# Attention and token mixer on one core: transposes in the scores' PSUM banks, half buffers for x and y, weight conversion in three stages

## The chip, the cores and the metric

The kernel runs on one core of one Trainium2 chip. The core has a matrix engine (TensorE, PE in the views), which reads SBUF and writes the eight banks of PSUM; VectorE (DVE) and ScalarE (ACT), which read PSUM and SBUF; GpSimd (POOL), which works in SBUF; and SyncE (SP), which here only issues DMAs. Each engine works through its own list of instructions in order. The metric is the device time of one execution in microseconds (us), and lower is better. Before the change it was 1676.6 us, the median of three runs (1676.05 to 1679.02).

## The reference

```python
def _attn_ref(q, k, v, g_q, g_k):            # q, k, v: (8, 12, 448, 64)
    def rmsnorm(x, g):
        return x / np.sqrt(np.mean(x * x, axis=-1, keepdims=True) + 1e-06) * g
    q_n, k_n = (rmsnorm(q, g_q), rmsnorm(k, g_k))
    scores = 1.0 / np.sqrt(q.shape[-1]) * np.matmul(q_n, k_n.transpose(0, 1, 3, 2))
    attn = np.exp(scores - np.max(scores, axis=-1, keepdims=True))
    attn = attn / (np.sum(attn, axis=-1, keepdims=True) + 1e-09)
    return np.matmul(attn, v)

# x: the heads side by side, (8, 448, 768); w_tok1 (448, 256), w_tok2 (256, 448),
# w_ch1 (768, 1536), w_ch2 (1536, 768)
def _moe_ref(x, w_tok1, w_tok2, w_ch1, w_ch2):
    xt = x.transpose(0, 2, 1)
    u = x + (np.maximum(xt @ w_tok1, 0.0) @ w_tok2).transpose(0, 2, 1)
    return u + np.maximum(u @ w_ch1, 0.0) @ w_ch2
```

All arithmetic is in float32. The four weight matrices arrive as float64, so the kernel first turns each into float32 by integer and float operations on the two 32-bit halves of every number.

## The kernel before

Work is in 8 batches. A batch's attention is 6 pairs of heads, and a pair has two steps of two 112-row chunks of keys each. For a pair, `load_qk` brings q and k, `norm_pair` makes the reciprocal root mean squares `rs` (ScalarE's squares, L553; VectorE's sums, L556; GpSimd's power, L561), `scale` multiplies q by them, and `trans_qk` (L212, L214) transposes q and k on TensorE into a PSUM bank and copies them out with ScalarE as `qkT`. A step computes four score tiles (L227), takes their exponentials on ScalarE (L233), multiplies those of the step before with v (L284) and adds the exponentials up (L270 on GpSimd, L274 on VectorE). `denominator` sums over partitions on TensorE (L298), and VectorE divides (L310 to L316). The result of a batch is `uT`, six blocks of 128 channels by 448 positions.

The mixer of a batch turns `uT` into `x` (`trans_x`, L364, copies L369 on ScalarE and L371 on VectorE by turns), multiplies with w_tok1 (`tok1`, L379) and w_tok2 (`tok2`, L387), adds to `uT` (L392), multiplies with w_ch1 (`ch1`, L403, 72 matmuls) and w_ch2 (`ch2`, L416, 72), adds again (L421), turns the result back into `y` (`trans_y`, L428, L430) and stores each half of `y` with a DMA that ScalarE issues (L435).

PSUM is split in three pools: four banks for score tiles (`ps_S`), two for products with v (`ps_O`), and two (`ps_M`) for everything else: transposes, denominators, and all the mixer's tiles. `x` and `y` share one buffer of a whole batch (`x_pool`, one slot, L358 to L436). So the copies into the next batch's `x` wait until the last half of `y` is stored.

The weights come in chunks of up to 128 by 256 numbers. `convert_first` (L136) splits a chunk on VectorE (L148, L149) and goes on with it on ScalarE (L151, L152). One item later `convert_last` (L154) finishes it on VectorE (L168, L170) and GpSimd (L172). The load of the chunk three items ahead is issued behind that (L126).

The order on TensorE, VectorE, ScalarE and GpSimd is written out by hand: `merge` (L23) weaves lists of items by their costs. In the first stage the attention of batch 0 (and two steps of batch 1) is woven with the first 15 conversion items; after that the attention of batch b + 1 is woven with the mixer of batch b, in batch 0 with the other conversions too (L474 to L483). The last batch's mixer has no attention beside it. Two versions of the program are built, and a test of g_q and g_k chooses one on the chip (L598). With these inputs it is the one that does not subtract a maximum.

```python
    m_tile = lambda: ps_M.tile([P, 512], F32, name="m_ps", tag="M")
    BEFORE = len(first) + NC + 1
    x_pool = pool("x_pool", 1)
```

## Time and profile before

| | |
|---|---|
| time, median of 3 runs | 1676.6 us (1676.05 to 1679.02) |
| the profiled execution | 1678.31 us, its span 1676.5 us |
| TensorE busy | 1539.9 us (92%) |
| VectorE, ScalarE, GpSimd busy | 473.2, 493.9, 368.6 us (28, 29, 22%) |
| mean granted TensorE clock | 0.97 of 2.4 GHz |
| from HBM, to HBM | 53.74 MB, 11.01 MB |

The page cuts the span in 40 slices of 42 us. TensorE is nearly full in most of them, and the three other engines are busy for half their time and more in the first seven, where the weights are converted. A busy share says where an engine works, not which wait ends last. For that, the views of waits and the timelines are read by stage: 15 to 124 us (attention of batch 0 beside conversions), 124 to 340 us (mixer of batch 0 beside attention and conversions), and from 340 us on (seven batches of about 200 us, the last shorter). A float32 matmul leaves two records in the trace, so the counts of TensorE's records are twice those of its matmuls.

### The profile page before, as it was taken

How to read it: one execution, taken by the hardware profiler on the slowest of the kernel's cores; microseconds unless marked ns; L12 is line 12 of the kernel's file. 1: busy time of each engine (PE TensorE's matmuls, PEld its weight loads, DVE VectorE, ACT ScalarE, POOL GpSimd, SP SyncE). 2: the span in 40 equal slices, each digit the busy share in tenths (PEclk: the TensorE clock that was granted, in tenths of full speed). 3: DMA queues.
4: the chain of work that ended last, by engine and by line, in shares of the span. 5: the costliest groups of instructions: out<-in, count | busy, mean ns of one | idle time of the engine just before them, and what ended most of it. 6: DMA issues, size and time to landing. Idle time of an engine off the chain costs nothing.

```text
span 1676.5 us, 13714 instructions
## 1 busy us (share of the span) xinstructions
PE 1539.9 (92%) x5248; PEld 734.3 (44%) x5248; DVE 473.2 (28%) x831; ACT 493.9 (29%) x890; POOL 368.6 (22%) x234
## 2 busy tenths in 40 slices
PE   5768998989998999989999899998999899998998
PEld 2234443444444444444444444444444444444554
DVE  4556866421222221122112221222122121111000
ACT  5554655323222222222222223222322222211100
POOL 5554554211211121111111211211122111100000
PEclk9879999999999999999999999999999999999999
DMA  5223433111002000110011101011100200000001
GB/s 121 79 78 98 123 105 109 53 33 29 22 17 61 17 22 17 44 39 17 17 28 39 33 17 28 23 33 33 28 22 18 61 17 12 6 17 17 0 0 34
DMA packets 119886, 65.73 MB, mean 39 GB/s; under 512 B 91716, under 2 KB 109892, under 8 KB 119812
## 3 DMA queue, kind: packets, MB, share of 16 engines
q1 hardware_dynamic: 111138, 53.53, 12.4%
q10 hardware_dynamic: 8674, 11.24, 2.2%
q8 instruction: 43, 0.70, 0.2%
q14 instruction: 31, 0.25, 0.0%
HBM read 53.74 MB, written 11.01 MB: 39 GB/s over the span
## 4 chain that ended last, share of the span: by engine, by line
PE 83%; DVE 6%; ACT 4%; DMA 3%; POOL 2%; issue 2%; SPq 0%; ACTq 0%; DVEq 0%; POOLq 0%
PE m_ps L416 26%; PE m_ps L403 24%; PE s_ps L227 9%; PE o_ps L284 9%; PE m_ps L379 5%; PE m_ps L387 4%; PE m_ps L298 2%; DMA out_dram<-y 2%; PE m_ps L364 2%; PE m_ps L212 1%; DVE uT L421 1%; ACT qkT L214 1%; POOL rs L561 1%; PE m_ps L428 1%; DVE es L274 1%
## 5 line engine op out<-in xcount | busy, mean ns | idle before, releaser
L416 PE MATMUL m_ps<-h,wc_sb 128*128 128x448 f32 x1152 | 455.8, 547 | 7.4 <-DVE uT L421 7.1
L403 PE MATMUL m_ps<-uT,wc_sb 128*128 128x448 f32 x1152 | 448.6, 543 | 4.1 <-ACT h L407 2.2
L403 PEld LDWEIGHTS m_ps<-uT,wc_sb 128*128 128x128 f32 x1152 | 213.8, 190 | 221.8 <-issue 203.5
L416 PEld LDWEIGHTS m_ps<-h,wc_sb 128*128 128x128 f32 x1152 | 213.8, 191 | 221.4 <-issue 207.5
L233 ACT ACTIVATE e<-s_ps,rs 112x448 f32<-112x448 f32 x384 | 211.9, 633 | 196.1 <-PE s_ps L227 196.1
L270 POOL TENSOR_TENSOR es<-e 112x896 f32<-112x896 f32 x48 | 100.2, 2087 | 765.5 <-PE m_ps L298 647.2
L227 PE MATMUL s_ps<-qkT 64*112 64x448 f32 x768 | 180.0, 590 | 27.6 <-ACT qkT L214 27.6
L561 POOL TENSOR_TENSOR rs<-ms,mhalf_c 112x16 f32<-112x16 f32 (+1 forms) x49 | 144.5, 2949 | 223.7 <-DVE ms L560 216.6
L284 PE MATMUL o_ps<-e,vt 112*64 112x448 f32 x768 | 170.6, 566 | 0.0
L310 DVE STREAM_TRANSPOSE dt<-m_ps 128x448 f32<-128x448 f32 x48 | 31.2, 650 | 452.3 <-PE m_ps L298 452.3
L407 ACT ACTIVATE h<-m_ps 128x448 f32<-128x448 f32 x96 | 52.1, 542 | 352.5 <-PE m_ps L403 352.5
L274 DVE TENSOR_TENSOR es<-es,e 112x896 f32<-112x896 f32 x96 | 113.7, 1185 | 82.5 <-ACT e L233 77.9
L421 DVE TENSOR_TENSOR uT<-uT,m_ps 128x448 f32<-128x448 f32 x48 | 29.8, 621 | 346.6 <-PE m_ps L416 346.4
L214 ACT ACTIVATE qkT<-m_ps,g_t 128x448 f32<-128x448 f32 x96 | 60.0, 631 | 220.7 <-PE m_ps L212 220.6
L227 PEld LDWEIGHTS s_ps<-qkT 64*112 64x112 f32 x768 | 64.4, 181 | 126.4 <-issue 93.6
L284 PEld LDWEIGHTS o_ps<-e,vt 112*64 112x64 f32 x768 | 47.9, 140 | 115.2 <-issue 115.2
L556 DVE TENSOR_REDUCE ms<-sq 112x16 f32<-112x1024 f32 (+1 forms) x49 | 58.5, 1196 | 138.0 <-ACT sq L553 138.0
L172 POOL TENSOR_TENSOR wc_sb<-m_t,e_t 128x256 f32<-128x256 f32 x72 | 62.5, 875 | 123.2 <-DVE e_t L170 122.1
L387 PE MATMUL m_ps<-w_sb,h 128*128 128x448 f32 x192 | 80.4, 564 | 8.3 <-DVE uT L392 4.6
L379 PE MATMUL m_ps<-x,w_sb 112*128 112x384 f32 x256 | 86.9, 497 | 0.0
L364 PE MATMUL m_ps<-ident,uT 128*112 128x128 f32 x192 | 40.7, 378 | 41.7 <-ACT x L369 36.8
L430 ACT COPY y<-m_ps 112x512 f32<-112x512 f32 x48 | 28.0, 585 | 168.4 <-PE m_ps L428 168.4
(45 smaller groups left out, 817.2 us busy)
## 6 DMA issues: line engine op xcount, KB each, us to landing
raw<-in_moe_w_ch_dram SPq DMA_DIRECT2D x72, 256.0 KB, 2.7
vt<-in_v_dram SPq DMA_DIRECT2D x48, 224.0 KB, 2.6
out_dram<-y ACTq DMA_DIRECT2D x16, 672.0 KB, 4.4
qk<-in_q_dram SPq DMA_DIRECT2D x92, 112.0 KB, 2.8
qk<-in_k_dram SPq DMA_DIRECT2D x92, 112.0 KB, 2.8
raw<-in_moe_w_tok_dram SPq DMA_DIRECT2D x4, 224.0 KB, 4.2
raw<-in_moe_w_tok_dram SPq DMA_DIRECT2D x2, 256.0 KB, 2.8
wc_sb<-in_q_dram SPq DMA_DIRECT2D x4, 112.0 KB, 3.8
```

Of the source, the lines that this page charges most:

```text
L214: nc.scalar.mul(st["qkT", p][:, i, :], ps[:, 0:S], g_t[:, i:i + 1])
L227: nc.tensor.matmul(out=ps[0:R, 0:S], lhsT=qkT[a * D:(a + 1) * D, 1, kc * R:(kc + 1) * R], rhs=qkT[a * D:(a + 1) * D, 0, :], start=True, st ...
L233: nc.scalar.activation(out=e[0:R, a, i, :], in_=pss[a][0:R, 0:S], func=AF.Exp, scale=st["rs", p][0:R, r:r + 1])
L270: nc.gpsimd.tensor_tensor(out=es[0:R], in0=e[0:R, :, 0, :], in1=e[0:R, :, 1, :], op=ALU.add)
L274: nc.vector.tensor_tensor(out=es[0:R], in0=es[0:R], in1=e[0:R, :, i, :], op=ALU.add)
L284: nc.tensor.matmul(out=o[a * D:(a + 1) * D, 0:S], lhsT=vt[0:R, a, kc * D:(kc + 1) * D], rhs=e[0:R, a, i, :], start=(kc == 0), stop=(kc == ...
L364: nc.tensor.transpose(ps[0:R, c * P:(c + 1) * P], st["uT", b][:, j, c * R:(c + 1) * R], ident[:, :])
L379: nc.tensor.matmul(out=ps[:, 0:HC], lhsT=w1_sb[0:R, c, jc * P:(jc + 1) * P], rhs=st["x"][0:R, c, cs], start=(c == 0), stop=(c == NS - 1))
L387: nc.tensor.matmul(out=ps[:, 0:S], lhsT=st["h1", jc][:, cc * P:(cc + 1) * P], rhs=w2_sb[:, jc].rearrange("p c r -> p (c r)"), start=(jc == ...
L403: nc.tensor.matmul(out=ps[:, 0:S], lhsT=wc1_sb[:, cc, f * P:(f + 1) * P], rhs=st["uT", b][:, cc, :], start=(cc == 0), stop=(cc == NC - 1))
L416: nc.tensor.matmul(out=ps[:, 0:S], lhsT=wc2_sb[:, f, cc * P:(cc + 1) * P], rhs=st["h2"][:, f, :], start=(f == 0), stop=(f == NF - 1))
L561: nc.gpsimd.tensor_tensor(out=rs[0:R, w], in0=ms[0:R, w], in1=self.mhalf_c[0:R].to_broadcast([R, (hi - lo) * n]), op=ALU.pow)
```

## The change

Transposes of q and k, of x and of y take their PSUM tiles from the four score banks (`s_tile`) instead of the two shared ones. `x` and `y` become tiles of half the channels, in two slots: half 0 of x, half 1 of x, half 0 of y, half 1 of y take them by turns. `trans_x` and `trans_y` share a helper, `turn`. The mixer now transposes the three blocks of a half and runs that half of tok1 before it goes on to the other half. In the last batch each block of 128 channels of `y` is stored by itself. A conversion is spread over three items: VectorE's split, an item later ScalarE's part, an item later VectorE's end and GpSimd's product. `cv_pool` has four slots instead of three, and loads are issued two items ahead instead of three.

```diff
@@ -60,12 +60,12 @@
     HC = C // 2
     HN = NS // 2
     assert S % NS == 0 and R <= P and 2 * D == P and H % 2 == 0 and NC == NPAIR
-    assert DT % P == 0 and C % P == 0 and DC % P == 0 and HC <= 512 and S <= 512
+    assert DT % P == 0 and C % P == 0 and DC % P == 0 and HC <= 512 and HC % P == 0 and S <= 512

     pool = lambda name, bufs, **kw: ctx.enter_context(tc.tile_pool(name=name, bufs=bufs, **kw))
     const = pool("const", 1)
     raw_pool = pool("raw_pool", 4)
-    cv_pool = pool("cv_pool", 3)
+    cv_pool = pool("cv_pool", 4)
     pre.qk_pool = pool("qk_pool", 3)
     pre.sq_pool = pool("sq_pool", 1)
     pre.st_pool = pool("st_pool", 4)
@@ -75,7 +75,7 @@
     es_pool = pool("es_pool", 1)
     rd_pool = pool("rd_pool", 2)
     uT_pool = pool("uT_pool", 2)
-    x_pool = pool("x_pool", 1)
+    x_pool = pool("x_pool", 2)
     h1_pool = pool("h1_pool", 2)
     h2_pool = pool("h2_pool", 1)
     ps_S = pool("ps_S", 4, space=PSUM)
@@ -90,6 +90,7 @@

     st = dict(pre.st)
     m_tile = lambda: ps_M.tile([P, 512], F32, name="m_ps", tag="M")
+    s_tile = lambda name: ps_S.tile([P, 512], F32, name=name, tag="S")

@@ -144,9 +145,17 @@
         m_t = cv_pool.tile([P, WCOLS], U32, name="m_t")
         st["cv", i] = e_t, m_t
         e, m = e_t[0:rows, 0:n], m_t[0:rows, 0:n]
-        mf = m.bitcast(F32)
         nc.vector.tensor_scalar(e, hi, 0x7FF00000, None, ALU.bitwise_and)
         nc.vector.tensor_scalar(m, hi, 0x000FFFFF, None, ALU.bitwise_and)
+
+    def convert_second(i):
+        rows, src, dst, split = chunks[i]
+        if src.dtype != I64:
+            return
+        e_t, m_t = st["cv", i]
+        n = src.shape[-1]
+        e, m = e_t[0:rows, 0:n], m_t[0:rows, 0:n]
+        mf = m.bitcast(F32)

         nc.scalar.activation(out=e, in_=e, func=AF.Relu, bias=expo_c[0:rows, 0:1], scale=8.0)
         nc.scalar.activation(out=mf, in_=m, func=AF.Identity, bias=one_c[0:rows, 0:1], scale=2.0**-20)
@@ -171,17 +180,17 @@
             out=e, in0=hi, scalar=0x80000000, in1=e, op0=ALU.bitwise_and, op1=ALU.bitwise_or)
         nc.gpsimd.tensor_tensor(out=dst, in0=fold(mf), in1=fold(ef), op=ALU.mult)

-    LOADS_AHEAD = 3
-
     def weight_items(lo, hi):

         def one(i):
             if i < len(chunks):
                 convert_first(i)
-            if i:
-                convert_last(i - 1)
-            if i + LOADS_AHEAD < len(chunks):
-                weight_load(i + LOADS_AHEAD)
+            if 0 <= i - 1 < len(chunks):
+                convert_second(i - 1)
+            if i >= 2:
+                convert_last(i - 2)
+            if i + 2 < len(chunks):
+                weight_load(i + 2)
         return [(1.0, lambda i=i: one(i)) for i in range(lo, hi)]


@@ -207,7 +216,7 @@
         qk = st["qk", p]
         if i == 0:
             st["qkT", p] = qkT_pool.tile([P, 2, S], F32, name="qkT")
-        ps = m_tile()
+        ps = s_tile("t_ps")
         for c in range(NS):
             nc.tensor.transpose(
                 ps[:, c * R:(c + 1) * R], qk[0:R, i, c].rearrange("p h d -> p (h d)"), ident[0:R, 0:R])
@@ -223,7 +232,7 @@
             kc = h * HN + i
             pss = []
             for a in range(2):
-                ps = ps_S.tile([P, 512], F32, name="s_ps")
+                ps = s_tile("s_ps")
                 nc.tensor.matmul(
                     out=ps[0:R, 0:S], lhsT=qkT[a * D:(a + 1) * D, 1, kc * R:(kc + 1) * R],
                     rhs=qkT[a * D:(a + 1) * D, 0, :], start=True, stop=True)
@@ -244,7 +253,7 @@
             st["e", p, i] = e_pool.tile([P, 2, HN, S], F32, name="e")
         for c in range(NS):
             for a in range(2):
-                ps = ps_S.tile([P, 512], F32, name="s_ps")
+                ps = s_tile("s_ps")
                 nc.tensor.matmul(
                     out=ps[0:R, 0:S], lhsT=qkT[a * D:(a + 1) * D, 0, c * R:(c + 1) * R],
                     rhs=qkT[a * D:(a + 1) * D, 1, :], start=True, stop=True)
@@ -355,20 +364,25 @@

-    def trans_x(b, j):
-
-        if j == 0:
-            st["x"] = x_pool.tile([P, NS, C], F32, name="x", tag="x")
-        ps = m_tile()
+    def turn(b, j, name, by_act):
+
+        half, o = divmod(j * P, HC)
+        if o == 0:
+            st[name, half] = x_pool.tile([P, NS, HC], F32, name=name, tag="x")
+        ps = s_tile("t_ps")
         for c in range(NS):
             nc.tensor.transpose(
                 ps[0:R, c * P:(c + 1) * P], st["uT", b][:, j, c * R:(c + 1) * R], ident[:, :])
         src = ps[0:R, :].rearrange("p (c n) -> p c n", c=NS)
-        dst = st["x"][0:R, :, j * P:(j + 1) * P]
-        if j % 2:
+        dst = st[name, half][0:R, :, o:o + P]
+        if by_act:
             nc.scalar.copy(out=dst, in_=src)
         else:
             nc.vector.tensor_copy(out=dst, in_=src)
+
+    def trans_x(b, j):
+
+        turn(b, j, "x", j % 2)

     def tok1(b, jc, h):
         cs = slice(h * HC, (h + 1) * HC)
@@ -377,7 +391,7 @@
         ps = m_tile()
         for c in range(NS):
             nc.tensor.matmul(
-                out=ps[:, 0:HC], lhsT=w1_sb[0:R, c, jc * P:(jc + 1) * P], rhs=st["x"][0:R, c, cs],
+                out=ps[:, 0:HC], lhsT=w1_sb[0:R, c, jc * P:(jc + 1) * P], rhs=st["x", h][0:R, c, :],
                 start=(c == 0), stop=(c == NS - 1))
         nc.scalar.activation(out=st["h1", jc][:, cs], in_=ps[:, 0:HC], func=AF.Relu)

@@ -421,26 +435,23 @@
             nc.vector.tensor_tensor(out=uT, in0=uT, in1=ps[:, 0:S], op=ALU.add)

     def trans_y(b, cc):
-        if cc == 0:
-            st["y"] = x_pool.tile([P, NS, C], F32, name="y", tag="x")
-        ps = m_tile()
-        for c in range(NS):
-            nc.tensor.transpose(
-                ps[0:R, c * P:(c + 1) * P], st["uT", b][:, cc, c * R:(c + 1) * R], ident[:, :])
-        nc.scalar.copy(
-            out=st["y"][0:R, :, cc * P:(cc + 1) * P], in_=ps[0:R, :].rearrange("p (c n) -> p c n", c=NS))
-        half = NC // 2
-        if cc % half == half - 1:
-            cs = slice((cc + 1 - half) * P, (cc + 1) * P)
+        turn(b, cc, "y", True)
+        half, o = divmod(cc * P, HC)
+        n = P if b == B - 1 else HC
+        if (o + P) % n == 0:
+            o += P - n
             nc.scalar.dma_start(
-                out=out[b].rearrange("(p c) n -> p c n", c=NS)[:, :, cs], in_=st["y"][0:R, :, cs])
-            if cc == NC - 1:
-                st.pop(("uT", b))
+                out=out[b].rearrange("(p c) n -> p c n", c=NS)[:, :, half * HC + o:half * HC + o + n],
+                in_=st["y", half][0:R, :, o:o + n])
+        if cc == NC - 1:
+            st.pop(("uT", b))

     def mlp_items(b):
         us = lambda n, cols: n * cols * 4 / 2400
-        items = [(0.5, lambda j=j: trans_x(b, j)) for j in range(NC)]
-        items += [(us(NS, HC), lambda j=j, h=h: tok1(b, j, h)) for j in range(NJ) for h in range(2)]
+        items = []
+        for h in range(2):
+            items += [(0.5, lambda j=j: trans_x(b, j)) for j in range(h * NC // 2, (h + 1) * NC // 2)]
+            items += [(us(NS, HC), lambda j=j, h=h: tok1(b, j, h)) for j in range(NJ)]
         items += [(us(NJ, S), lambda cc=cc: tok2(b, cc)) for cc in range(NC)]
         items += [(us(NC // 2, S), lambda f=f, p=p: ch1(b, f, p)) for f in range(NF) for p in range(2)]
         early, late = items, []
@@ -458,10 +469,10 @@
     first, second, third = weight_chunks()
     chunks = first + second + third
     AHEAD = 1
-    BEFORE = len(first) + NC + 1
+    BEFORE = len(first) + NC + 2

     load_v(0)
-    for i in range(LOADS_AHEAD):
+    for i in range(2):
         weight_load(i)
     scale(0)
     trans_qk(0, 0)
@@ -476,7 +487,7 @@
     for b in range(B):
         early, late = mlp_items(b)
         if b == 0:
-            early = merge(early, weight_items(BEFORE, len(chunks) + 1))
+            early = merge(early, weight_items(BEFORE, len(chunks) + 2))
         lo = (b + AHEAD) * per + 2
         att = att_items(lo, lo + per) if b + AHEAD < B else []
         for _, fn in merge(att, early + late):
```

At the boundary between two batches (here from the second to the third) TensorE's list had, before, from the last matmuls of ch2 to the end of tok1 (L212 transposes of q and k, L428 of y, L364 of x; then L227 scores, L284 products with v, L298 denominators, L379 tok1):

```order
L416 MATMUL m_ps<-h_3328,wc_sb 128x448 x9
L212 MATMUL m_ps<-ident,qk 128x112 x4
L428 MATMUL m_ps<-ident,uT 112x128 x4
L212 MATMUL m_ps<-ident,qk 128x112 x4
L428 MATMUL m_ps<-ident,uT 112x128 x4
L364 MATMUL m_ps<-ident,uT 112x128 x24
L227 MATMUL s_ps<-qkT 112x448 x4
L284 MATMUL o_ps<-e,vt 64x448 x4
L298 MATMUL m_ps<-es,one_c 64x448 x2
L379 MATMUL m_ps<-x,w_sb 128x384 x16
```

Now the same place reads (L221 transposes of q and k, L374 those of y and of x, L236 scores, L293 products, L307 denominators, L393 tok1):

```order
L430 MATMUL m_ps<-h_3333,wc_sb 128x448 x9
L221 MATMUL t_ps<-ident,qk 128x112 x4
L374 MATMUL t_ps<-ident,uT 112x128 x4
L221 MATMUL t_ps<-ident,qk 128x112 x4
L374 MATMUL t_ps<-ident,uT 112x128 x16
L393 MATMUL m_ps<-x,w_sb 128x384 x4
L236 MATMUL s_ps<-qkT 112x448 x4
L293 MATMUL o_ps<-e,vt 64x448 x4
L307 MATMUL m_ps<-es,one_c 64x448 x2
L393 MATMUL m_ps<-x,w_sb 128x384 x4
L374 MATMUL t_ps<-ident,uT 112x128 x12
L393 MATMUL m_ps<-x,w_sb 128x384 x8
```

The transposes of y and the first three of x stand in one run of 16 instructions, a quarter of tok1 follows at once, and the last three blocks of x stand behind the attention step and the second quarter of tok1.

On VectorE the distance between the two parts of a conversion shows by the buffers' numbers. In the first stage before, with L148 and L149 the split and L168 and L170 the end:

```order
L148 TENSOR_SCALAR e_t_455<-raw_314 128x192
L149 TENSOR_SCALAR m_t_456<-raw_314 128x192
L168 SCALAR_TENSOR_TENSOR m_t_406<-raw_283,m_t_406 128x256
L170 SCALAR_TENSOR_TENSOR e_t_405<-raw_283,e_t_405 128x256
L274 TENSOR_TENSOR es_443<-es_443,e_466 112x896 x2
L148 TENSOR_SCALAR e_t_504<-raw_365 128x256
L149 TENSOR_SCALAR m_t_505<-raw_365 128x256
L168 SCALAR_TENSOR_TENSOR m_t_456<-raw_314,m_t_456 128x192
L170 SCALAR_TENSOR_TENSOR e_t_455<-raw_314,e_t_455 128x192
```

Now, with L177 and L179 the end:

```order
L323 STREAM_TRANSPOSE rd_532<-rc_530 128x448
L325 TENSOR_TENSOR uT_326<-o_ps_472,rd_532 128x448
L148 TENSOR_SCALAR e_t_535<-raw_445 128x192
L149 TENSOR_SCALAR m_t_536<-raw_445 128x192
L177 SCALAR_TENSOR_TENSOR m_t_437<-raw_358,m_t_437 128x192
L179 SCALAR_TENSOR_TENSOR e_t_436<-raw_358,e_t_436 128x192
L567 TENSOR_REDUCE ms_549<-sq_548 112x16
L571 TENSOR_SCALAR ms_549<-ms_549 112x16
L148 TENSOR_SCALAR e_t_576<-raw_486 128x256
L149 TENSOR_SCALAR m_t_577<-raw_486 128x256
L177 SCALAR_TENSOR_TENSOR m_t_478<-raw_396,m_t_478 128x256
L179 SCALAR_TENSOR_TENSOR e_t_477<-raw_396,e_t_477 128x256
```

Before, chunk 455 was split in one item and ended in the next (L168 and L170 on `e_t_455`). Now the first item ends chunk 436, and the chunk split there, 535, is not yet ended in the second item, which ends 477.

## Rows read from the trace of the kernel before

**Rows 1.** The page, part 2: busy tenths and granted clock in 40 slices.

```profile
PE   5768998989998999989999899998999899998998
PEclk9879999999999999999999999999999999999999
```

**Rows 2.** TensorE's waits, 15 to 124 us: total us, times, longest.

```profile
PE s_ps L227 <- ACT qkT L214: 27.6, 7, 6.6
```

**Rows 3.** Windows, first stage: busy us (records) of each engine, PEclk, DMA, GB/s.

```profile
26.58:116.70 90.12, 61.89 (x265) 22.58 (x265) 52.46 (x100) 48.96 (x92) 51.51 (x32) 0.85 0.31 83
...
54.06:70.46 16.40, 10.07 (x45) 3.58 (x45) 10.24 (x21) 8.79 (x17) 11.92 (x8) 0.84 0.36 90
```

**Rows 4.** Timeline of one pair: start, us, engine, line, operation, [idle before <-releaser].

```profile
46.12 1.76 PE L227 MATMUL s_ps<-qkT 64*112 64x448 f32 x8
...
49.77 0.26 DVE L148 TENSOR_SCALAR e_t<-raw 128x192 uint32<-128x192 uint32 x1
...
50.06 0.45 ACT L151 ACTIVATE e_t<-e_t,expo_c 128x192 uint32<-128x192 uint32 x1 [4.56 <-DVE e_t L148]
...
50.77 2.19 ACT L233 ACTIVATE e<-s_ps,rs 112x448 f32<-112x448 f32 x4
...
52.83 1.17 ACT L214 ACTIVATE qkT<-m_ps,g_t 128x448 f32<-128x448 f32 x2
...
54.06 2.34 PE L227 MATMUL s_ps<-qkT 64*112 64x448 f32 x8 [3.61 <-ACT qkT L214]
```

**Rows 5.** TensorE's waits, 124 to 340 us.

```profile
PE m_ps L212 <- ACT qkT L214: 9.0, 3, 6.0
PE m_ps L428 <- DVE uT L421: 5.4, 2, 5.1
PE m_ps L387 <- DVE uT L392: 4.6, 2, 2.4
```

**Rows 6.** Windows, two stretches at the low clock.

```profile
294.00:301.00 7.00, 4.41 (x12) 2.91 (x13) 5.83 (x14) 3.27 (x9) 2.69 (x3) 0.51 0.22 56
256.50:263.30 6.80, 3.94 (x9) 2.31 (x10) 3.29 (x9) 2.86 (x6) 2.46 (x3) 0.50 0.50 135
```

**Rows 7.** TensorE's waits, 340 us to the end.

```profile
PE m_ps L364 <- ACT x L369: 35.4, 7, 5.6
PE m_ps L212 <- ACT qkT L214: 8.7, 12, 0.7
PE m_ps L416 <- DVE uT L421: 6.1, 22, 0.3
PE m_ps L387 <- ACT qkT L214: 3.6, 5, 0.7
PE m_ps L428 <- DVE uT L421: 2.5, 8, 0.3
```

**Rows 8.** Timeline, a batch boundary, with a score matmul ahead of it.

```profile
524.48 1.76 PE L227 MATMUL s_ps<-qkT 64*112 64x448 f32 x8
...
537.44 1.44 PE L364 MATMUL m_ps<-ident,uT 128*112 128x128 f32 x8
...
538.20 0.58 ACTq L435 DMA_DIRECT2D out_dram<-y  x1
...
543.14 0.58 ACT L369 COPY x<-m_ps 112x512 f32<-112x512 f32 x1 [4.96 <-DMA out_dram<-y]
...
543.77 3.84 PE L364 MATMUL m_ps<-ident,uT 128*112 128x128 f32 x16 [4.90 <-ACT x L369]
...
547.55 2.98 PE L227 MATMUL s_ps<-qkT 64*112 64x448 f32 x8
...
552.86 10.59 PE L379 MATMUL m_ps<-x,w_sb 112*128 112x384 f32 x32
```

**Rows 9.** The page, part 6: DMAs, KB each, median us to landing.

```profile
vt<-in_v_dram SPq DMA_DIRECT2D x48, 224.0 KB, 2.6
out_dram<-y ACTq DMA_DIRECT2D x16, 672.0 KB, 4.4
```

## The prediction

> **What bounds the kernel now.** I read the page first, then TensorE's waits in three stretches, then one timeline in each stretch where a wait is long. The page says that TensorE is busy for 92% of the span, and its clock row, which shows where it is not at its best, has its lowest digits in the first eighth [rows 1]. So TensorE bounds the kernel, and what can be gained is its idle time and the time it spends at 1.2 GHz instead of 2.4.
>
> From 15 to 124 us (attention of batch 0 with the first weight conversions) 27.6 us go to one wait: the score matmul L227 for ScalarE's qkT copy, seven times [rows 2]. The timeline of one pair shows why that copy is late [rows 4]. The scores of the second half start at 46.12 us, but their exponentials start only at 50.77. In front of them on ScalarE stands the conversion L151, which waited 4.56 us for VectorE's L148 of the same chunk, issued at 49.77 behind the denominators' work. The copy then runs at 52.83 and the next scores at 54.06, after 3.61 us of idle. From 26.58 to 116.70 us, six pairs take 90.12 us, 15.0 each, with TensorE busy for 61.89 and a mean granted clock of 0.85 [rows 3].
>
> From 124 to 340 us (batch 0's mixer with the rest of the conversions) the waits are shorter and of another kind: transposes L212 and L428 wait for a bank of the two-bank pool to be read out, and tok2's L387 for VectorE [rows 5].
>
> From 340 us on the batches repeat every 200 us. There one wait dominates: transposes of x, L364, 35.4 us in 7 waits; the rest are waits for the same two banks, 0.2 to 0.7 us each [rows 7]. At the boundary the last store of y goes out at 538.20 us, the copies into x start at 543.14 since x and y are one buffer, and the third block's transposes start at 543.77 after 4.90 us of idle. They then run at 1.2 GHz: 16 records take 3.84 us where 8 took 1.44 before the stall, and the scores behind take 2.98 where they take 1.76 elsewhere [rows 8].
>
> **Part 1: half buffers and the new order at the boundary.** Half 0 of x takes the slot of y's half 0, whose store went out several matmul groups earlier, so the first three copies wait for no DMA. Half 1 waits for the store of y's half 1, which landed 5 us after its issue (538.20 to 543.14). What lies between now, by the order: the transposes of x, one tok1 group, scores, products, denominators, the second tok1 group. A tok1 group is 8 of the 32 records that take 10.59 us, so 2.6 us [rows 8]; two of them are 5.3 us already, and that also covers batch 7, which has no attention between. The 35.4 us of waiting go. Late next are the copies themselves: tok1 now follows directly on three transposes instead of behind scores and products, so TensorE waits for the last copy of a half, 0.58 us and some 0.3 of hand-over, in each half: 1.8 us at each of 7 boundaries, 12.6 in all. Net 35.4 - 12.6 = 23. If the clock then stays at 2.4 GHz, the 16 transposes save about 1 us (3.84 against at most 2 x 1.44) and the scores 1.2. That is 2.2 us at this boundary. The low stretch need not fall on the same work at each of them, so I count 1.6 as the mean: 7 x 1.6 = 11. Bounds: 12 (the copies of each half cost 3 us and the clock still falls: 35.4 - 7 x 3.3) and 46 (no new wait).
>
> **Part 2: transposes in the four score banks.** From 340 us on the waits for the two banks are L212 8.7, L416 6.1, L428 2.5, L387 3.6 and smaller ones, 22.7 in all. They exist because a mixer tile holds one bank and all else takes turns on the other. With transposes elsewhere, the mixer's tiles alternate. These go but for what the score banks cost. Scores need four of four banks, and a transposed tile holds one until its copy (about 0.6 us) is done. In the order, matmuls of the mixer stand between most transposes and the next scores, and for qkT the scores need the copy anyway. I take 20, between 5 (each of 24 tiles a batch adds 0.1) and 23. In 124 to 340 us the same waits are L212 9.0 and L428 5.4, the longest 6.0 and 5.1 [rows 5]. They are long since the reader stands behind conversions. A freed bank moves the wait to the next user, which comes 4 to 7 us of matmuls later, so most of it is covered: 10 of 14.4. tok2's 4.6 stays. Two of the low-clock stretches follow such waits, 6.80 and 7.00 us with 3.94 and 4.41 us of busy TensorE [rows 6], which would be half as long at full clock: 4. Together 14, between 4 and 21.
>
> **Part 3: conversions in three stages.** The instructions stay the same in number: two of VectorE, two of ScalarE, two of VectorE, one of GpSimd for each chunk. Only the distance grows by one item, and the load is issued two items ahead instead of three, behind the same release. ScalarE no longer meets a chunk that VectorE began in the same item, so the exponentials of the pair shown could start at about 46.6 instead of 50.77, the qkT copy directly behind the transposes, and the scores some 3 us sooner. What then bounds a pair? Over the six pairs VectorE is busy for 52.46 us, GpSimd 51.51 and ScalarE 48.96 [rows 3]: 8.2 to 8.7 a pair. TensorE's 10.3 a pair includes records at half clock. Four engines near 9 us that feed each other will not overlap perfectly. Floor 8.7, ceiling 12.5 (today's TensorE time plus 2 us of waits); I take 11, nearer to TensorE's row: 6 x (15.0 - 11) = 24, between 15 and 38. The shorter lead of the loads costs nothing while a weight load lands in about the 2.6 us of a v load [rows 9] and an item comes every 3 us or more. In bursts it could show, and that is inside the ceiling.
>
> GpSimd's spans grow where VectorE works beside it: in the pair from 54.06 to 70.46 GpSimd is busy for 11.92 us against the mean of 8.6 [rows 3]. The Trainium skill (GPSIMD Engine Reference, 1. Specifications) says that GpSimd's SBUF interfaces are shared with VectorE and contended by VectorE instructions with two SBUF inputs. By that rule a denser stage makes both slower, and the first rival below would be right; the trace agrees as far as the 11.92 goes.
>
> **Part 4: the end.** The last store is a sixth of a result, 448 x 128 x 4 bytes = 229 KB, instead of half of one. The stores of 672 KB landed in 4.4 us, the loads of 224 KB in 2.6 [rows 9], so 1.8 sooner. Five more issues on ScalarE lie beside matmuls, at no cost. Bounds 0 and 2.
>
> **Sum.** 23 + 11 + 20 + 14 + 24 + 2 = 94 us. The profiled execution took 1678.3 us (span 1676.5), 1.7 above the median of 1676.6. 1678.3 - 94 = 1584; set against the median, 1583.
>
> **Rivals.**
> First: the conversions stay the bound. The staggering removes ScalarE's wait, but VectorE and GpSimd, packed closer, slow each other, and a pair falls only to about 13.5 us, the 11.92 of GpSimd plus hand-overs. For it speaks the 54.06 row; against it the other pairs' lower sums. Part 3 then gives 6 x 1.5 = 9, and part 2's early share 5: 94 - 15 - 9 = 70, or 1607. Chance 0.2.
> Second: the boundary is not cleared. The short waits for copies, with transposes between them, still let TensorE's clock fall, and x's half 1 gets there just as its store lands. Part 1 gives 12 instead of 34: 1605. For it: the clock fell at the boundary shown. Against: those were stalls of some 5 us, up to 5.6 [rows 7]. Chance 0.12.
> Third, on the other side: the score banks become the bottleneck. Each of 24 transposed tiles a batch (12 of q and k, 6 of x, 6 of y), 192 in all, holds a bank that TensorE wants next, and in order it stands behind it. A whole copy each, 0.6 us, costs 115 us: 1583 + 115 = 1698. It decides from 94 / 192 = 0.5 us a tile on. For it: four score tiles do need every bank. Against: the order puts matmuls of 2 us and more between. Chance 0.04.
> That the change does nothing: the waits go but their time returns elsewhere, with all terms at their lower ends at once and a new cost besides. Chance 0.02.
>
> **How the numbers follow.** The forecast, 1583, has a chance of 0.62; its own range is 1562 to 1605. With the first two rivals inside, and part 3 and part 1 each near its better end below, I give 1550 to 1625; outside lie the last two cases and a sum of lower or of upper ends. A measurement of this kernel can tell 0.2% from nothing, 3.4 us. Faster by more: 0.62 + 0.2 + 0.12 = 0.94; within: 0.02; slower: 0.04.
>
> **What would show it.** Right: the wait of x's transposes for a store is gone from TensorE's waits; a batch in the middle takes about 191 us instead of 199.8; the granted clock stays at 2.4 GHz across the boundaries; transposes wait for no copy; six pairs of the first stage take about 66 us, and ScalarE's L151 waits for VectorE hardly at all; the last store lands within 3 us. Wrong: score matmuls waiting for banks held by t_ps, which would be the third rival; a pair at 13 us or more with GpSimd or VectorE nearly full, the first; a low clock behind each boundary, the second.

## Result and profile after

| | before | after |
|---|---|---|
| time, median of 4 runs each, same chip | 1677.15 us (1676.05 to 1679.02) | 1545.57 us (1545.49 to 1546.39) |
| span of the profiled execution | 1676.5 us | 1543.7 us |
| TensorE busy | 1539.9 us (92%) | 1489.2 us (96%) |
| mean granted TensorE clock | 0.97 | 0.996 |

The ratio is 0.9215, with a 95% interval of 0.92 to 0.9231: 131.6 us less. The forecast was 1583 us, in a range from 1550 to 1625. The direction was right and the time came out 4.4 us under the low end of the range: the change gave 131.6 us where the sum had 94.

The first view is the page's second part. These rows answer to [rows 1].

```profile
PE   5879999999999999999999999999999999999998
...
PEclk9999999999999999999999999999999999999999
```

From the fourth slice on TensorE is at 90% or more but for the last slice, and no slice is left with a clock below 9 tenths. The next view is TensorE's waits over the whole span after the change (total us, times, longest); it answers to [rows 2, 5, 7].

```profile
PE t_ps L221 <- POOL wc_sb L212: 13.2, 1, 13.2
PE m_ps L393 <- ACT x L379: 11.2, 13, 1.8
PE s_ps L236 <- ACT qkT L223: 9.4, 8, 2.0
PE m_ps L393 <- DVE x L381: 8.2, 3, 6.4
PE m_ps L401 <- DVE uT L406: 2.5, 2, 2.4
PE m_ps L307 <- DVE es L283: 1.7, 2, 1.0
PE m_ps L430 <- DVE dt L319: 1.5, 1, 1.5
PE t_ps L374 <- DVE uT L435: 0.6, 2, 0.4
```

The first row is the start, which the change leaves as it was. Gone are the 35.4 us in which x's transposes waited for a store, and nearly all waits of a transpose or a mixer tile for a bank: the last four rows hold 6.3 us in all. The score matmuls wait 9.4 us in all. New are tok1's waits for the copies of x (L393), as the prediction had them, at 0.7 to 0.9 us in each half; one of them, 6.4 us in batch 0, is new in another way (the experiment with all copies of batch 0 on ScalarE).

The windows of the first stage give the stretch, its length, the busy us (records) of PE, PEld, DVE, ACT and POOL, then the granted clock, DMA share and GB/s. This one is the kernel after, six pairs, and answers to the first of [rows 3].

```profile
25.29:85.40 60.11, 52.33 (x276) 20.91 (x276) 54.47 (x100) 50.51 (x95) 48.30 (x31) 1.00 0.45 117
```

A pair takes 10.0 us instead of 15.0, with the same work on VectorE (54.47 against 52.46) and on ScalarE, and TensorE's clock is never low. VectorE, at 91% of the window, is now the fullest engine there.

At the batch boundary the timeline of the kernel after answers to [rows 8] (start, us, engine, line and operation, in brackets the idle before and what ended it).

```profile
474.34 1.91 PE L374 MATMUL t_ps<-ident,uT 128*112 128x128 f32 x16
...
475.87 0.58 ACTq L443 DMA_DIRECT2D out_dram<-y  x1
...
476.55 0.59 ACT L379 COPY x<-t_ps 112x512 f32<-112x512 f32 x1 [0.70 <-PE t_ps L374]
...
477.19 1.24 PE L393 MATMUL m_ps<-x,w_sb 112*128 112x384 f32 x3 [0.93 <-ACT x L379]
```

The sixteen transposes, four of y and twelve of x, run on at full clock (1.91 us where [rows 8] had 3.84 behind the stall), x's copies wait for no DMA, and TensorE waits 0.93 us for the last of them. A batch in the middle takes 186.7 us (tok1 starts at 290.52, 477.19, 663.88 us) instead of 199.8; the prediction had 191.

### The profile page after: what moved, and what is told of

Its sections match the earlier page's. It is cut to its first block, busy times and chain, and to the rows that moved or that the text cites. A ratio compares the mean times of both kernels' runs of the same rounds, so it can differ in the third digit from the quotient of the medians.

```text
span 1543.7 us, 13746 instructions
## 1 busy us (share of the span) xinstructions
PE 1489.2 (96%) x5248; PEld 715.6 (46%) x5248; DVE 470.8 (30%) x831; ACT 489.9 (32%) x890; POOL 369.7 (24%) x234
## 4 chain that ended last, share of the span: by engine, by line
PE 88%; DVE 4%; DMA 2%; ACT 2%; POOL 1%; issue 1%; SPq 0%; ACTq 0%; DVEq 0%; POOLq 0%
PE m_ps L417 28%; PE m_ps L430 26%; PE s_ps L236 10%; PE o_ps L293 9%; PE m_ps L393 5%; PE m_ps L401 4%; PE m_ps L307 2%; PE t_ps L221 2%; PE t_ps L374 2%; DMA raw<-in_moe_w_ch_dram 1%; POOL rs L572 1%; ACT qkT L223 1%; DVE e_t L148 1%; DVE m_t L149 1%; DVE es L283 1%
## 5 line engine op out<-in xcount | busy, mean ns | idle before, releaser
L430 PE MATMUL m_ps<-h,wc_sb 128*128 128x448 f32 x1152 | 450.4, 542 | 1.5 <-DVE dt L319 1.5
L236 PE MATMUL s_ps<-qkT 64*112 64x448 f32 x768 | 171.7, 567 | 9.4 <-ACT qkT L223 9.4
L293 PE MATMUL o_ps<-e,vt 112*64 112x448 f32 x768 | 165.5, 552 | 0.0
L223 ACT ACTIVATE qkT<-t_ps,g_t 128x448 f32<-128x448 f32 x96 | 58.8, 632 | 206.6 <-PE t_ps L221 206.3
L236 PEld LDWEIGHTS s_ps<-qkT 64*112 64x112 f32 x768 | 62.1, 174 | 107.6 <-issue 87.6
L393 PE MATMUL m_ps<-x,w_sb 112*128 112x384 f32 x256 | 91.1, 506 | 19.4 <-ACT x L379 11.2
L293 PEld LDWEIGHTS o_ps<-e,vt 112*64 112x64 f32 x768 | 46.6, 136 | 108.8 <-issue 108.8
L379 ACT COPY y<-t_ps 112x512 f32<-112x512 f32 x48 | 28.0, 585 | 156.6 <-PE t_ps L374 156.6
L393 PEld LDWEIGHTS m_ps<-x,w_sb 112*128 112x128 f32 x256 | 47.8, 194 | 57.0 <-ACT x L379 16.6
```

The costliest lines, as they stand in the source:

```text
L223: nc.scalar.mul(st["qkT", p][:, i, :], ps[:, 0:S], g_t[:, i:i + 1])
L236: nc.tensor.matmul(out=ps[0:R, 0:S], lhsT=qkT[a * D:(a + 1) * D, 1, kc * R:(kc + 1) * R], rhs=qkT[a * D:(a + 1) * D, 0, :], start=True, st ...
L293: nc.tensor.matmul(out=o[a * D:(a + 1) * D, 0:S], lhsT=vt[0:R, a, kc * D:(kc + 1) * D], rhs=e[0:R, a, i, :], start=(kc == 0), stop=(kc == ...
L393: nc.tensor.matmul(out=ps[:, 0:HC], lhsT=w1_sb[0:R, c, jc * P:(jc + 1) * P], rhs=st["x", h][0:R, c, :], start=(c == 0), stop=(c == NS - 1))
L430: nc.tensor.matmul(out=ps[:, 0:S], lhsT=wc2_sb[:, f, cc * P:(cc + 1) * P], rhs=st["h2"][:, f, :], start=(f == 0), stop=(f == NF - 1))
```

## Experiments

**One part at a time.** The first three kernels are the kernel before with one part of the change each; the fourth is the changed kernel with the conversions put back to two stages. The kernel before was timed again beside them each time; its medians lie between 1676.3 and 1678.0 us.

Only the transposes' banks (x, y, q and k):

```diff
+    s_tile = lambda name: ps_S.tile([P, 512], F32, name=name, tag="S")
...
-        ps = m_tile()
+        ps = s_tile("t_ps")
```

> The kernel before with one edit: transposes of q and k, x and y take their PSUM tiles from the four score banks. Theory A (a wait of TensorE costs its idle row and about 0.26 us more, because the pipeline of weight loads and matmuls drains and must start again; the last block of the kernel fell from 10.00 to 9.46 us where the idle row said 0.28): some 65 short waits from 340 us on give 22.7 us of idle rows and 17 of restarts, 2.8 plus 2.5 a batch, and the mixer of batch 0 some 14: about 1623 us, a batch about 194.5 instead of 199.8. Theory B (a wait costs its idle row; what was won beyond the sum of 94 comes from the three parts helping each other): 1677 - 22.7 - 14 = 1640, a batch about 197. The store wait of some 5 us at each boundary stays in both.

Measured: 1606.99 us (1606.33 to 1608.65), the kernel before beside it 1676.3; ratio 0.9589 [0.9573, 0.9605], 69.3 us. More than either theory gave. The store wait stayed as it was.

Only the half buffers and the order at the boundary:

```diff
-    x_pool = pool("x_pool", 1)
+    x_pool = pool("x_pool", 2)
...
+        items = []
+        for h in range(2):
+            items += [(0.5, lambda j=j: trans_x(b, j)) for j in range(h * NC // 2, (h + 1) * NC // 2)]
+            items += [(us(NS, HC), lambda j=j, h=h: tok1(b, j, h)) for j in range(NJ)]
```

> The kernel before with the half buffers for x and y and the new order at the boundary alone; transposes stay in the two shared banks, the conversions and the last stores as before. Both theories: the store wait goes. Theory A: the clock holds across the boundaries and the gain is 35.4 of idle, some 15 of low clock and 7 x 0.3 of restarts, less new waits for copies of 3 us a boundary in only two banks: 1677 - 53 + 21 = 1645. Theory B: the short waits behind the transposes let the clock fall as long as the banks are two, so that only idle time is won: 1677 - 35 + 21 = 1663.

Measured: 1646.68 us (1646.13 to 1648.24), ratio 0.9822 [0.9806, 0.9838], 29.6 us. Near theory A. The buffers and the order were not tried apart.

Only the three-stage conversions, with the four slots of `cv_pool` and the loads two items ahead that belong to them:

```diff
-            if i:
-                convert_last(i - 1)
+            if 0 <= i - 1 < len(chunks):
+                convert_second(i - 1)
+            if i >= 2:
+                convert_last(i - 2)
```

> The kernel before with the three-stage conversions alone. Theory A: the wait of the score matmuls for qkT came from ScalarE's head-of-line wait alone, so the first stage wins its 30 us without the other parts, pairs of about 10 us, and the mixer of batch 0 wins a few: 1677 - 35 = 1642. Theory B: with transposes in the two shared banks a pair stays near 12.5 us, since the second transpose waits for a bank: 1677 - 16 = 1661. From 340 us on nothing changes in both.

Measured: 1643.09 us (1641.75 to 1645.68), ratio 0.9806 [0.979, 0.9823], 33.2 us. Theory A by the time, and ScalarE's waits show its mechanism. These are its waits for VectorE's split (total us, times, longest), in five pairs of the kernel before (26.58 to 102.90 us) and then in the same five pairs here (25.56 to 75.75 us).

```profile
ACT e_t L151 <- DVE e_t L148: 30.4, 10, 4.7
```

```profile
ACT e_t L159 <- DVE e_t L147: 1.6, 2, 1.1
```

The changed kernel without the three-stage conversions (the last diff taken back):

> The changed kernel with the conversions in two stages as before. Theory A: parts add up, so it loses what the conversions give alone, some 35 us: 1546 + 35 = 1581. Theory B: the parts help each other, so leaving one out loses more than it gives alone: 1600 or above.

Measured: 1578.45 us (1577.0 to 1579.85), ratio 0.9419 [0.9403, 0.9435], 32.9 us slower than the changed kernel. So the conversions are worth the same with and without the other parts.

69.3 + 29.6 + 33.2 = 132.1, against 131.6 for the whole. The parts add up, so the sum can be checked term by term: the banks were forecast at 34 and gave 69, the conversions 24 and 33, the boundary 34 and 30.

**Where the banks' 69 us come from.** These windows cut the span where tok1 of batch 0 and of batch 1 starts. Kernel before:

```profile
123.82:353.03 229.21, 203.03 (x677) 95.91 (x676) 139.78 (x321) 109.95 (x224) 95.37 (x83) 0.94 0.34 94
353.03:1676.50 1323.47, 1258.98 (x4246) 606.02 (x4244) 267.75 (x382) 319.81 (x549) 203.08 (x101) 0.99 0.09 24
```

The same two stretches of the kernel with only the banks moved:

```profile
118.52:326.07 207.55, 196.10 (x676) 92.50 (x676) 140.95 (x322) 109.65 (x224) 97.01 (x86) 0.98 0.38 106
326.07:1604.70 1278.63, 1241.24 (x4246) 604.23 (x4244) 268.00 (x382) 316.91 (x549) 207.13 (x101) 0.99 0.10 25
```

From the second tok1 on, 44.8 us are saved: TensorE's idle time falls from 64.5 to 37.4 (27.1), and its busy time by 17.7, with the same 4246 records and the same granted clock of 0.99. The clock does not account for the 17.7: the stretches at the low clock there hold 26.1 us of TensorE's busy time in the kernel before and 26.9 us with the banks moved. The prediction looked at the idle time only. To see whether the busy time belongs to the banks' waits, two kernels move one kind of transpose each.

Only x and y in the score banks (the edit above in `trans_x` and `trans_y`, not in `trans_qk`):

> The kernel before with only the transposes of x and y in the score banks; those of q and k stay in the two shared ones. From 340 us on the waits that name y's transposes or the add behind them (L416, L428) are 35 with 10.4 us of idle rows; in batch 0's mixer 6.4 us. Theory A (each wait costs its idle row and some 0.25 us of restart): 10.4 + 9 + 6.4 = 26 us, so about 1650; in the last batch a block of w_ch2 falls from 10.00 to 9.46 us. Theory B (idle rows only): 17 us, 1659; a block falls to 9.72.

Measured: 1654.28 us (1651.21 to 1655.09), the kernel before beside it 1678.03; ratio 0.9855 [0.9838, 0.9871], 23.8 us. By the time that is between the two, nearer to A's gain than to B's; the distance of the blocks below decides for A.

The last batch shows one such wait by itself: a w_ch2 block of 24 records, four transposes of y, the next block, with nothing else on TensorE. First the timeline of TensorE in the kernel before.

```profile
1628.77 9.29 PE L416 MATMUL m_ps<-h,wc_sb 128*128 128x448 f32 x24 [0.28 <-DVE uT L421]
1637.89 0.60 PE L428 MATMUL m_ps<-ident,uT 128*112 128x128 f32 x4
1638.77 9.29 PE L416 MATMUL m_ps<-h,wc_sb 128*128 128x448 f32 x24 [0.28 <-DVE uT L421]
```

And the same place with x and y moved to the score banks:

```profile
1607.12 9.19 PE L417 MATMUL m_ps<-h,wc_sb 128*128 128x448 f32 x24
...
1616.58 9.19 PE L417 MATMUL m_ps<-h,wc_sb 128*128 128x448 f32 x24
...
1626.03 9.19 PE L417 MATMUL m_ps<-h,wc_sb 128*128 128x448 f32 x24
```

From start to start it is 10.00 us with the wait and 9.46 without: one wait costs 0.54 us, of which its row shows 0.28. Of the other 0.26, the block itself is 0.10 longer (9.29 against 9.19). The rest is lost overlap: without a wait the next group starts before the record of the transposes has ended, as in this timeline of TensorE in the changed kernel:

```profile
1498.58 9.19 PE L430 MATMUL m_ps<-h,wc_sb 128*128 128x448 f32 x24
1507.61 0.60 PE L374 MATMUL t_ps<-ident,uT 128*112 128x128 f32 x4
1508.04 9.19 PE L430 MATMUL m_ps<-h,wc_sb 128*128 128x448 f32 x24
```

Here 0.60 us of transposes take 0.43 of the engine's time (1507.61 to 1508.04). This is counted as busy time, so the waits' view can't show it. (The ends of matmuls are modelled in these records; the distance from start to start is not.)

Only q and k in the score banks (the same edit in `trans_qk` alone):

> The kernel before with only the transposes of q and k in the score banks. Their own waits from 340 us on (L212 12, L387 5) are 12.3 us in idle rows, in batch 0's mixer 9.0, and 4 us of low clock behind the long ones. Theory A: 12.3 + 4.3 + 9 + 4 = 30 us, 1646. Theory B: 25 us, 1651. If the two halves of the PSUM part add up to much less than its 69 us, the waits are shared: each kind of transpose alone keeps the two banks busy enough.

Measured: 1637.25 us (1636.3 to 1640.55), ratio 0.9764 [0.9748, 0.978], 40.8 us. Beyond theory A, and the wait of x's and y's side stays, as this row of TensorE's waits in that kernel shows:

```profile
PE m_ps L417 <- DVE uT L422: 11.1, 26, 4.0
```

In this kernel the last batch's blocks again stand 10.00 us apart (1588.02, 1598.02, 1608.02).

From the second tok1 on, the two kernels repeat what the banks together showed. With x and y moved TensorE has 35 waits less there and its busy time falls by 10.0 us (0.29 a wait); with q and k moved it has 36 less and 8.7 us (0.24 a wait). Together the halves give 64.6 of 69.3. What only both give lies between the first two tok1: 21.7 us with both, 10.5 with q and k alone, and a loss of 1.1 with x and y alone. There the wait moves on to the transposes of q and k, as this row of TensorE's waits in the kernel with x and y moved shows:

```profile
PE m_ps L213 <- DVE uT L422: 3.3, 1, 3.3
```

**The end.** The changed kernel with stores by halves in the last batch too:

```diff
-        n = P if b == B - 1 else HC
+        n = HC
```

> The changed kernel with the last batch's result stored in two halves, as before. The last store lands in 4.4 us instead of 2.9: 1.5 us later. Rival: the six fine stores cost ScalarE's issues and gain nothing: the same time within 0.5 us.

Measured: 1546.87 us (1545.98 to 1548.43), ratio 0.9219 [0.9203, 0.9234], 1.3 us above the changed kernel, with overlapping ranges. The size fits (a last store lands in 2.9 us instead of 4.4), but it is too small to be told from nothing.

**Trying to take away what is late next.** The changed kernel with x of the next batch transposed sooner: the first half ahead of the last w_ch2 block, the second behind the first quarter of tok1.

```diff
+        items += [tok(0, 0)] + turn_x(b, 1) + [tok(j, 0) for j in range(1, NJ)]
...
+            if cc == NC - 1 and b + 1 < B:
+                late += turn_x(b + 1, 0)
```

> The changed kernel with the first three blocks of the next batch's x transposed ahead of the last block of w_ch2, and the other three behind the first quarter of tok1 and not behind the second. It should remove TensorE's last regular waits, for copies into x, 0.93 and 0.68 us at each of 7 boundaries. Theory A (restart included): 7 x (1.61 + 0.5) = 15 us, 1531. Theory B: 11 us, 1535. Rival: the second half's tiles stand in score banks until y's store has landed, and the scores behind them wait: no gain, 1546 or above.

Measured: 1566.91 us (1566.25 to 1567.73), ratio 0.9338 [0.9323, 0.9354], 21 us slower than the changed kernel. TensorE's waits of this kernel have a row that no other kernel has:

```profile
PE s_ps L236 <- ACT x L379: 12.0, 6, 2.5
```

And its timeline at the boundary shows why.

```profile
483.58 0.58 ACTq L443 DMA_DIRECT2D out_dram<-y  x1
...
485.08 1.48 PE L374 MATMUL t_ps<-ident,uT 128*112 128x128 f32 x12
...
486.48 1.00 PE L236 MATMUL s_ps<-qkT 64*112 64x448 f32 x2
489.20 1.07 ACT L379 COPY x<-t_ps 112x512 f32<-112x512 f32 x2 [3.44 <-DMA out_dram<-y]
...
489.84 2.58 PE L236 MATMUL s_ps<-qkT 64*112 64x448 f32 x5 [2.36 <-ACT x L379]
```

Three transposed tiles of x hold three of the four score banks, and their copies wait for y's store of 483.58. The scores get one bank and stop. Five records then take 2.58 us, where eight take 1.76 at full clock, and the mean clock of the run is 0.984. This is the rival of the expectation, at a higher price than it named, and the mechanism of the prediction's third rival, brought about by order alone.

The same with only the first half moved, the second left where the change puts it:

```diff
+        items = (turn_x(b, 0) if b == 0 else []) + tok(0) + turn_x(b, 1) + tok(1)
...
+            if cc == NC - 1 and b + 1 < B:
+                late += turn_x(b + 1, 0)
```

> The changed kernel with the first half of the next batch's x transposed ahead of the last w_ch2 block of the batch before; the second half stays where the change puts it, behind the two token products of the first half. Theory A (at each of the seven batch boundaries the changed kernel shows two idle rows L393<-x, 0.9 us for the first half and 0.7 us for the second, and a restart costs about 0.25 us more than its idle row): the first of the two goes, 7 x (0.93 + 0.25) = 8 us, about 1538 us. Theory B (what the kernel with both halves moved showed, 1567 us: score banks are held by x tiles whose copies wait for a store of y): it was moving the first half that did it, and the time is 1555 us or more, with rows L236<-ACT x in the waits.

Measured: 1545.54 us (1541.37 to 1547.46), ratio 0.9217 [0.9201, 0.9233]: no difference from the changed kernel. Neither theory: the score matmuls wait for no x, and the first half's wait is gone, but the second half's has grown. The timeline of this kernel behind the boundary:

```profile
484.30 1.52 PE L374 MATMUL t_ps<-ident,uT 128*112 128x128 f32 x12
...
486.06 0.62 DVE L325 TENSOR_TENSOR uT<-o_ps,rd 128x448 f32<-128x448 f32 x1
486.60 0.68 DVE L381 COPY x<-t_ps 112x512 f32<-112x512 f32 x1
...
487.43 4.75 PE L393 MATMUL m_ps<-x,w_sb 112*128 112x384 f32 x14 [1.60 <-DVE x L381]
```

The transposes of the second half now follow the denominators directly, since the tok1 quarter that stood between has moved up. VectorE's copy of x stands behind the division of the pair's result (L325) and ends later. 1.60 us is what 0.93 and 0.68 were together: the wait moved on, whole.

The changed kernel with all x copies of batch 0 on ScalarE:

```diff
-        turn(b, j, "x", j % 2)
+        turn(b, j, "x", b == 0 or j % 2)
```

> The changed kernel with all six x copies of batch 0 on ScalarE, in place of three on VectorE. Theory A (the wait of 6.4 us before the first token product, at 85 to 91.5 us, is VectorE's queue: x copies stand there behind weight conversions and exp sums, while ScalarE has gaps of 3 us): the wait falls to 2 us or less and the clock does not fall to 1.2 GHz from 89.5 to 96.3 us, together 4 to 7 us, about 1540 us. Theory B (the weights' conversion, on all three engines, sets when batch 0 can go on, so that a token product that starts earlier only waits later): 1544 to 1547 us, with a new wait on a conversion between 90 and 120 us.

Measured: 1540.59 us (1538.3 to 1543.32), ratio 0.9188 [0.9173, 0.9204], 5.0 us below the changed kernel. Theory A. The windows of the changed kernel at this place, where tok1 of batch 0 waits:

```profile
85.40:91.50 6.10, 0.00 (x0) 0.01 (x1) 5.87 (x13) 1.81 (x4) 5.91 (x3) 0.85 0.47 117
89.50:96.30 6.80, 4.78 (x8) 2.52 (x8) 3.54 (x10) 0.91 (x2) 4.19 (x5) 0.51 0.42 114
```

And with the copies on ScalarE:

```profile
85.40:91.50 6.10, 4.09 (x8) 2.25 (x8) 4.60 (x11) 2.40 (x6) 5.91 (x4) 0.72 0.54 123
89.50:96.30 6.80, 6.80 (x26) 2.67 (x25) 2.49 (x7) 4.23 (x9) 3.52 (x5) 0.87 0.44 112
```

In the changed kernel TensorE stands for the whole 6.10 us while VectorE is busy for 5.87 of it, with ScalarE at 1.81; then the clock is at 0.51. On ScalarE the copies end sooner, and TensorE's wait there is 2.36 us. The clock still falls, but for less work: in the whole run TensorE is busy at the low clock for 3.4 us, where the changed kernel has 8.4.

Both edits together:

> The last two edits together. Theory A: they are at different places and add up, about 1532 us, or 1540 where only the one at batch 0 pays. Theory B: neither pays, 1546 us or more.

Measured: 1537.13 us (1535.91 to 1538.48), ratio 0.9167 [0.9153, 0.9181]. It is the fastest of all, 140.7 us below the kernel before, and lies between the two numbers of theory A. That the first half's move gives 3.5 us here and nothing alone is within what the two intervals overlap; whether it does is left open.

## Why the prediction was right or wrong

**The step that failed: part 2, the size of a bank wait.** The prediction added up what the rows of [rows 5, 7] say: "22.7 in all", of which "I take 20", and "Together 14" for 124 to 340 us. The kernel with the banks alone gave 69.3 us. The two profiled spans differ by 71.8: by the windows, 44.8 of them lie from the second tok1 on, 21.7 between the first two, and 5.3 ahead of the first, where the prediction put nothing. It took the idle row for the whole price of a wait; the runs showed that TensorE's busy time pays some two thirds as much again (17.7 beside 27.1 us in the late stretch).

- Late stretch, 44.8 for 20. Besides the store's, [rows 7] show 20.9 us in 47 waits, and the same view has five smaller rows (below), 5.4 us in 19. That is 26.3 us; the prediction's 22.7 left out 3.6 of it (both rows of L403 and one of L364), and the 2.7 that it took off for the score banks hardly came. The block distance says that each wait costs 0.26 more than its row: 66 x 0.26 = 17, together 43. Measured were 27.1 of idle and 17.7 of busy time, with as much work at the low clock as before. That 0.26 was measured at the w_ch2 blocks alone; that the other users pay as much is an estimate, which the fall of the busy time by 17.7 bears out, and so do its parts with x and y or q and k alone. The upper bound of 23 was no bound, since it took the idle rows for the whole price.
- Middle stretch, 21.7 for 14: idle fell from 26.2 to 11.5, 14.7 where 10 were counted, and busy time by 6.9, with the granted clock up from 0.94 to 0.98. Most of the 6.9 is the clock, where 4 were counted: the stretches at the low clock hold 9.8 us of busy time instead of 21.2, and half of the difference is 5.7. The guess that a part of the freed waits comes back at other users held: new waits of the score matmuls hold 3.7 us, where 4.4 were allowed for. What the idle sum missed is that tok2's wait (L387), taken to stay at 4.6, fell to 2.9, and that smaller rows of the two banks went as well (L416 1.0, L403 0.7).
- First stretch, 5.3 for 0: the prediction counted the banks only from 124 us on, though transposes of q and k need them there too. The stretches at the low clock hold 18.5 us of busy time there instead of 29.3. That part was not taken further.

The smaller rows of TensorE's waits in the kernel before, 340 us to the end:

```profile
PE m_ps L403 <- DVE uT L392: 1.9, 6, 0.3
PE m_ps L403 <- ACT h L407: 1.5, 6, 0.2
PE m_ps L428 <- ACT y L430: 1.5, 5, 0.3
PE m_ps L416 <- ACT y L430: 0.3, 1, 0.3
PE m_ps L364 <- ACT y L430: 0.2, 1, 0.2
```

**Part 3, the conversions: mechanism right, size low.** 33 us, for 24 (bounds 15 to 38). ScalarE's wait for VectorE's split went, as forecast: 30.4 us in 10 waits, then 1.6 in 2. The prediction took 11 us a pair, by TensorE's 10.3 a pair at partly halved clock; measured are 10.0, and with the stalls gone the clock is 1.00. With the conversions alone tok1 of batch 0 starts 30.0 us earlier (93.80 for 123.82), and another 7.5 us go between the first two tok1, where the prediction counted nothing for this part (from 229.2 to 221.7). Behind that 1.3 are lost; these are the profiled spans, 36.2 apart, where the medians give 33.2.

The windows of the same five pairs let the first rival be judged. Before, then with the conversions alone:

```profile
26.58:102.90 76.32, 51.81 (x221) 18.77 (x221) 44.64 (x85) 41.19 (x77) 43.75 (x27) 0.84 0.31 82
```

```profile
25.56:75.75 50.19, 42.59 (x221) 16.40 (x221) 45.42 (x84) 41.87 (x79) 40.63 (x26) 1.00 0.42 111
```

VectorE's busy time rises by 0.8 us and GpSimd's falls by 3.1 with one record less, although the same work stands in two thirds of the time. So packing them closer did not slow them in sum. Single instructions moved both ways: GpSimd's eight products for the token weights (tile w_sb) fell from 1304 to 722 ns each, while its powers (tile rs) rose from 3.23 to 3.44 us and VectorE's small step ahead of them (L560) from 331 to 851 ns. The rival's premise, 11.92 us of GpSimd for a pair, was a single pair's: it holds 8 GpSimd records, where the six pairs hold 5.3 in the mean, and four of them are such products at 1558 ns. The prediction read the 11.92 as slower work alone. TensorE's busy time falls by 9.2 us with the same 221 records, as the clock goes from 0.84 to 1.00. The rule of the Trainium skill (GPSIMD Engine Reference, 1. Specifications) that GpSimd's SBUF interfaces are shared with VectorE and contended is not refuted by this, but here it set no bound.

**Part 1, the boundary: mechanism right, the total near the forecast in part by luck.** 29.6 us, for 34. The store wait of 35.4 went, and tok1's waits for copies came, 13.1 us in that kernel where 12.6 were foreseen. The clock gave more than the 11 counted: at the seven boundaries of the kernel before, the stretches at the low clock (0.50) hold 29.4 us of TensorE's busy time, so half of that, 14.7, is an estimate of what the clock cost; with the half buffers alone no matmul runs at the low clock from 345.31 us on. These three make 37. Two costs that the sum did not have took some 7 of it back. In batch 0 the first w_ch1 matmul starts 3.5 us later (165.79 for 162.31). And busy time came back from w_ch1 of batch 1 on. These windows begin there, first in the kernel before, then with the half buffers alone:

```profile
378.28:1676.50 1298.22, 1234.78 (x4164) 593.56 (x4164) 258.48 (x368) 313.77 (x539) 197.04 (x98) 0.99 0.09 25
```

```profile
377.52:1646.44 1268.92, 1226.13 (x4164) 584.21 (x4164) 258.47 (x368) 313.50 (x539) 197.09 (x98) 1.00 0.10 25
```

TensorE's busy time falls by 8.7 us there, although the six low stretches in it had cost 13.1; so 4.4 came back with 12 new waits beside. That these pay some 0.4 us each beyond their rows is an estimate from this difference, and was not tried by itself.

The second rival did not happen: in the changed kernel the window from the second tok1 to the end has a granted clock of 1.00.

```profile
290.52:1543.70 1253.18, 1236.14 (x4276) 598.89 (x4276) 269.32 (x383) 320.81 (x555) 207.31 (x101) 1.00 0.10 27
```

**Part 4, the end:** 1.3 us measured, not told from nothing, for 2.

**The third rival** did not happen in the changed kernel, which has no row of a score matmul waiting for a t_ps tile. It is real all the same: the kernel with both halves of x moved brought it about, with twelve transposes ahead of a store's landing.

**The range** stopped at 1550 since both ends of part 2 came from idle rows. The restarts in the late stretch alone (43 for 20) would have given 1583 - 23 = 1560. By the single kernels, part 2 gave 35 us more than forecast and part 3 gave 9 more, part 1 gave 4 less and part 4 gave 1 less. That is 39 more, where the whole change gave 38 more (131.6 for 94). Without part 2's excess the time would have lain in the range.

## What to carry to other kernels

A short wait of the bounding engine can cost more than its idle row: compare the distance from start to start of the same block with and without a wait, and multiply the difference by the number of waits. Here a matmul tile and a transposed tile that took turns at the same two banks paid it at each change; score banks that stood idle then were a good place for the transposes, as long as no copy out of them waited for a DMA. When the wait for the last of several things is removed, look for what ends next: at the boundary 0.93 us came back whole behind another instruction.

## What the runs showed of the hardware

- A wait of 0.28 us of TensorE for a PSUM bank lengthened a block of 12 float32 matmuls and 4 transposes by 0.54 us (10.00 against 9.46). Part of it, 0.10, is in the block's own busy time.
- VectorE and GpSimd packed into two thirds of the time did the same work in about the same busy time (45.42 against 44.64 and 40.63 against 43.75 us), with single instructions faster or slower.
- In the changed kernel TensorE's granted clock fell after a wait of 6.41 us (0.51 from 89.50 to 96.30 us) and, in batch 0 again, after one of 2.36 us (0.50 from 127.25 to 130.66 us), and stayed at 1.00 over the waits of 0.7 to 0.9 us at the seven boundaries.
- A store of 224 KB landed in 2.9 us and one of 672 KB in 4.4.
